# Turning the second group of v by DMA transposes instead of on TensorE, in a fused cross-covariance attention and feed-forward kernel

## The chip, the cores and the metric

The kernel runs on one core of a Trainium2 chip. A core has five engines with an instruction queue each: TensorE (PE, with weight loads of its own, PEld), VectorE (DVE), ScalarE (ACT), GpSimd (POOL) and SyncE (SP). SP only issues DMAs and waits; ACT and POOL issue DMAs too. All queues feed the same 16 DMA engines. An instruction starts when its engine has come to it and the semaphores that it waits for have been raised, so a waiting instruction holds up all that stands behind it on the same engine.

The metric is the device time of one execution in microseconds (us). Before the change it is 720.22 us, the median of three runs (720.19 to 720.47).

## The reference

B = 4 batches of N = 6080 rows and C = 256 channels; the feed-forward part has 2048 hidden units. Cut to what matters:

```python
qn = q / (norm(q, axis=1) + 1e-6);  kn = k / (norm(k, axis=1) + 1e-6)
s = kn.transpose(0, 2, 1) @ qn / tau          # (B, 256, 256): channels by channels
a = exp(s - s.max(-1));  a /= a.sum(-1) + 1e-9
x = (v @ a).reshape(B * N, 256)
h = x @ w_in                                   # (24320, 2048)
out = (s_ * maximum(h, 0)**2 + b_) @ w_out     # (24320, 256)
```

The scores are over channels, so a batch has one 256 x 256 matrix `a`, for which all rows of its q and k are read first. All of q, k, v and out are float32 in memory; the kernel computes in float16 with float32 sums.

## The kernel before

The kernel folds each batch's `a` into w_in: `wa = a @ w_in` (256 x 2048, held in float16), so that the hidden layer is `v @ wa` and x is never made. The 24,320 rows of v are cut into 48 groups of 512 rows (the last one has 256). A group needs `vT`, its rows turned so that channels lie on the partitions, since TensorE contracts over partitions.

**Before the steps (0 to 39 us).** POOL loads q and k of batch 0 in chunks, casting to float16 on the way; PE sums the scores (`Gram.mm`, L142), ACT and DVE square and fold for the norms. Then come w_in in three parts, v of group 0, v of group 1 (L418), the four parts of w_out (L424), v of group 2 (L426), and two scalars, all on POOL's queue. `keep_busy` (L438) gives PE idle products while it waits for loads. The softmax of batch 0 and the first part of its fold into w_in follow, and group 0's v is turned on PE (`transpose_v(0)`, L464).

**The steps.** The main loop (L797) has 48 x 16 steps and a tail; step s belongs to group s // 16. In a step PE multiplies one 128-wide block of `wa` with the group's `vT` (`mm1`, L605: two matmuls of 512 columns, into `h_ps`, of which there are two buffers of two blocks each). At every second step ACT applies the relu (L615) to two blocks. The squares (L626 on ACT, L628 on DVE) make `g`. The second product of a group runs some steps later among the first products of the next one: for group 0 and the last one plainly (`plain_mm2`, L677, group 0's from step 11 on), for the others with seven products in place of eight (L773), which needs sums of w_out's blocks (`combine_w`, L492 to L498) and of g's (`sums_of`, L699 to L705).

**Side work.** `at_step(s, f)` hangs a piece of work behind step s (L513); after the products and relus of a step all that hangs there is issued, in the order in which it was hung (L829). The first lines that use it place the rest of batch 0's fold (L521), the casts of w_out (L530, steps 7, 14, 18 and 24), the row sums of w_out (L532), and the loads of v (L540): groups 3 and 4 at step 2, group 5 at step 18, then one a group. The next batches' q and k, their scores, norms and softmax hang there as well (L546 to L572). The order on each engine is the order of issue: `po` keeps it.

**How v is turned.** There are two ways in the code. `transpose_v` (L366) has PE turn eight 128 x 128 blocks into a PSUM tile of the pool `ps_o` (three buffers, shared with the second products), and DVE copies them to `vT` (L374). `crossbar_v` (L377) has SP issue four DMA transposes (L383), each of which turns 128 rows of 256 channels straight into `vT`. Group 0 goes by the first way ahead of the steps, group 1 by the first way at step 12, and every group g from 2 on by the second way at step (g - 2) * 16 + 6. Since SP has hardly anything else to do, a transposing DMA is issued as soon as its v has landed and its `vT` is free, however late the step is at which it hangs.

**Buffers.** `v16` has four (`vpool`), `vT` three (`vtpool`). A buffer goes to the next load when the one that held it is released. POOL's DMAs take turns on eight semaphores, so that a load is issued when the one eight before it has landed.

Of the kernel before, what the change touches and what calls it, by code (L numbers as in the profile page):

```python
# [16 lines left out]
def kernel(  # L17
# [36 lines left out]
    def po(ins):  # L54

        tc.keep_in_program_order(ins)
        return ins
# [294 lines left out]
    def group(g):  # L352
        t0 = g * TG
        return t0, min(TG, NT - t0) // P
# [3 lines left out]
    def load_v(g):  # L358
        t0, nj = group(g)
        v16 = vpool.tile([P, TG // P, C], FP16, tag="v16", name="v16")  # L360
        po(nc.gpsimd.dma_start(  # L361
            out=v16[:, :nj, :],
            in_=v_flat[t0 : t0 + nj * P, :].rearrange("(p j) c -> p j c", j=nj)))
        v_tiles[g] = v16

    def transpose_v(g):  # L366
        _, nj = group(g)
        v16 = v_tiles.pop(g)
        vT_ps = ps_o.tile([P, CH, TG], FP16, tag="o_ps", name="vT_ps")
        for j in range(nj):  # L370
            for ch in range(CH):
                po(nc.tensor.transpose(vT_ps[:, ch, ts(j, P)], v16[:, j, ts(ch, P)], ident16))
        vT = vtpool.tile([P, CH, TG], FP16, tag="vT", name="vT")
        po(nc.vector.tensor_copy(out=vT[:, :, : nj * P], in_=vT_ps[:, :, : nj * P]))  # L374
        vT_tiles[g] = vT

    def crossbar_v(g):  # L377

        _, nj = group(g)
        v16 = v_tiles.pop(g)  # L380
        vT = vtpool.tile([P, CH, TG], FP16, tag="vT", name="vT")
        for j in range(nj):
            po(nc.sync.dma_start_transpose(out=vT[:, :, ts(j, P)], in_=v16[:, j, :]))  # L383
        vT_tiles[g] = vT
# [128 lines left out]
    def at_step(s, f):  # L513
        side.setdefault(int(s), []).append(f)
# [23 lines left out]
    for g in range(NG):  # L538
        if g >= 3:
            at_step(max(g - 4, 0) * FT + 2, lambda g=g: load_v(g))  # L540
        if g >= 1:
            if g == 1:
                at_step(12, lambda g=g: transpose_v(g))
            else:
                at_step((g - 2) * FT + 6, lambda g=g: crossbar_v(g))
    for b in range(1, B):  # L546
# [250 lines left out]
    for s in range(NS + FT):  # L797
        g, m = divmod(s, FT)
# [66 lines left out]
```

## Time and profile before

| what | value |
|---|---|
| median of three runs | 720.22 us |
| the profiled execution's own time | 720.22 us |
| its span, first to last instruction | 718.5 us |
| PE busy | 699.4 us, 97% |
| DVE busy | 625.9 us, 87% |
| ACT busy | 544.5 us, 76% |
| eight PE transposes of group 1 (L372) | from 48.49 us, 219 ns each, pipelined |
| DVE's copy of them (L374) | 49.13 us, 0.69 us |
| step 16, the first use of group 1's vT (L605) | 51.10 us |
| DMA transposes (L383) | 182, median 3.2 us from issue to landing, 2.3 to 8.7 |
| POOL's DMA queue (q0) | 26,064 packets, 43.40 MB |
| SP's DMA queue (q1) | 63,072 packets, 38.43 MB |

A row of the timeline gives start, duration, engine, line, operation, what is written and read, and, in brackets, how long the engine had been idle and what released it. PE's matmuls overlap: the duration of one is longer than the distance to the next, so the distance (the pitch) is what it costs. For a DMA the time to landing counts from its issue to the last of its 16 completion marks. "SPq" stands for SP's queue, whose rows are the issues, not the transfers. The trace also holds a record for each packet of a DMA, with its queue, start, duration and size.

### The profile page before, as it was taken

How to read it: one execution, taken by the hardware profiler on the slowest of the kernel's cores; microseconds unless marked ns; L12 is line 12 of the kernel's file. 1: busy time of each engine (PE TensorE's matmuls, PEld its weight loads, DVE VectorE, ACT ScalarE, POOL GpSimd, SP SyncE). 2: the span in 40 equal slices, each digit the busy share in tenths (PEclk: the TensorE clock that was granted, in tenths of full speed). 3: DMA queues.
4: the chain of work that ended last, by engine and by line, in shares of the span. 5: the costliest groups of instructions: out<-in, count | busy, mean ns of one | idle time of the engine just before them, and what ended most of it. 6: DMA issues, size and time to landing. Idle time of an engine off the chain costs nothing.

```text
span 718.5 us, 17642 instructions
## 1 busy us (share of the span) xinstructions
PE 699.4 (97%) x7481; PEld 505.0 (70%) x7481; DVE 625.9 (87%) x879; ACT 544.5 (76%) x588; POOL 109.8 (15%) x189
## 2 busy tenths in 40 slices
PE   4799999999999999999999999999999999999998
PEld 3556777776677777777677777777668777777777
DVE  4779999998889999999888899999887888888886
ACT  4489877887777777788777777778877777777875
POOL 4532332201201222111110222110000000000000
PEclk9999999999999999999999999999999999999999
DMA  9999999547565979443973777844423333321202
GB/s 237 207 259 148 172 166 149 110 103 134 103 105 120 153 133 144 105 96 75 152 155 63 139 136 125 154 93 83 105 65 75 92 71 74 97 59 46 83 30 75
DMA packets 89791, 84.27 MB, mean 117 GB/s; under 512 B 59664, under 2 KB 64848, under 8 KB 89712
## 3 DMA queue, kind: packets, MB, share of 16 engines
q0 software_dynamic: 26064, 43.40, 37.7%
q1 hardware_dynamic: 63072, 38.43, 21.5%
q8 instruction: 59, 0.97, 0.5%
q10 hardware_dynamic: 576, 1.31, 0.5%
q14 instruction: 20, 0.16, 0.1%
HBM read 78.91 MB, written 24.90 MB: 144 GB/s over the span
## 4 chain that ended last, share of the span: by engine, by line
PE 92%; DMA 4%; ACT 1%; DVE 1%; POOL 0%; issue 0%; ACTq 0%; POOLq 0%
PE h_ps L605 45%; PE o_ps L773 40%; PE s_ps L142 4%; PE wa_ps L309 2%; DMA qk<-in_q_dram 2%; DMA qk<-in_k_dram 1%; DMA w_in<-in_moe_w_in_dram 1%; ACT r L615 1%; PE o_ps L651 0%; POOL qk L126 0%; PE o_ps L677 0%; ACT g L626 0%; PE idle_ps L442 0%; DVE o_sb L633 0%; DVE sq L162 0%
## 5 line engine op out<-in xcount | busy, mean ns | idle before, releaser
L615 ACT ACTIVATE r<-h_ps 128x1024 f16<-128x1024 f32 (+1 forms) x384 | 387.6, 1013 | 146.9 <-PE h_ps L605 145.0
L605 PE MATMUL h_ps<-vT,wa 128*128 128x512 f16 (+7 forms) x1632 | 451.9, 364 | 0.6 <-ACT r L615 0.4
L773 PEld LDWEIGHTS <-S 128*128 128x128 f16 x2944 | 197.9, 98 | 85.1 <-DVE S L699 0.4
L773 PEld LDWEIGHTS <-g 128*128 128x128 f16 x2208 | 155.0, 98 | 74.1
L628 DVE TENSOR_TENSOR g<-r 128x2048 f16<-128x2048 f16 (+2 forms) x150 | 174.7, 1165 | 15.1 <-ACT r L615 14.9
L773 PE MATMUL o_ps<-T,S 128*128 128x128 f16 x2208 | 183.2, 219 | 0.3 <-DVE S L699 0.2
L605 PEld LDWEIGHTS <-wa 128*128 128x128 f16 x1632 | 136.0, 98 | 21.4 <-issue 1.0
L773 PE MATMUL o_ps<-w_out,g 128*128 128x128 f16 x1472 | 134.2, 219 | 0.3 <-DVE u L633 0.3
L633 DVE SCALAR_TENSOR_TENSOR o_sb<-o_ps,s_out,u 128x256 f32<-128x256 f32 x138 | 66.4, 481 | 47.6 <-PE o_ps L773 45.1
L626 ACT ACTIVATE g<-r 128x1024 f16<-128x1024 f16 (+1 forms) x97 | 100.4, 1035 | 0.2
L142 PE MATMUL s_ps<-qk 128*128 128x256 f16 (+1 forms) x384 | 70.0, 283 | 14.0 <-ACT qk L133 8.7
L361 POOL DMA_DIRECT2D v<-in_v_dram x48 | 31.3, 656 | 263.0 <-DMA vT<-v 199.5
L633 DVE SCALAR_TENSOR_TENSOR u<-o_ps,s_out,rowconst 128x256 f32<-128x256 f32 x138 | 65.9, 478 | 0.0
L773 PE MATMUL o_ps<-w_out,S 128*128 128x128 f16 x736 | 63.4, 219 | 0.0
L773 PE MATMUL o_ps<-N,g 128*128 128x128 f16 x736 | 63.4, 219 | 0.0
L188 POOL DMA_DIRECT2D f<-f x30 | 26.3, 877 | 225.8 <-DVE f L178 167.0
L165 ACT ACTIVATE sq<-qk 128x1024 f16<-128x1024 f16 (+3 forms) x49 | 50.4, 1033 | 10.3 <-DMA qk<-in_k_dram 6.3
L701 DVE TENSOR_TENSOR S<-S,g 128x2048 f16<-128x2048 f16 (+1 forms) x47 | 56.4, 1201 | 1.3
L699 DVE TENSOR_TENSOR S<-g 128x2048 f16<-128x2048 f16 (+1 forms) x47 | 56.0, 1192 | 0.0
L705 DVE TENSOR_TENSOR S<-g,S 128x2048 f16<-128x2048 f16 x46 | 55.9, 1216 | 0.0
L703 DVE TENSOR_TENSOR S<-g 128x2048 f16<-128x2048 f16 x46 | 55.9, 1215 | 0.0
L142 PEld LDWEIGHTS <-qk 128*128 128x128 f16 (+1 forms) x384 | 32.9, 101 | 19.8 <-DVE qk L132 8.1
(75 smaller groups left out, 324.3 us busy)
## 6 DMA issues: line engine op xcount, KB each, us to landing
out_dram<-o_sb SPq DMA_DIRECT2D x46, 512.0 KB, 3.0
v<-in_v_dram POOLq DMA_DIRECT2D x47, 256.0 KB, 4.7
qk<-in_k_dram POOLq DMA_DIRECT2D x42, 256.0 KB, 6.0
qk<-in_q_dram POOLq DMA_DIRECT2D x42, 256.0 KB, 7.2
f<-f POOLq DMA_DIRECT2D x30, 128.0 KB, 3.0
vT<-v SPq DMA_TRANSPOSE x182, 3.2
w<-in_moe_w_out_dram POOLq DMA_DIRECT2D x4, 512.0 KB, 11.4
raw<-in_q_dram ACTq DMA_DIRECT2D x2, 512.0 KB, 6.6
```

The costliest lines, as they stand in the source:

```text
L142: po(nc.tensor.matmul(self.s_ps[:, ch, :], kc[:np_, j, ts(ch, P)], qc[:np_, j, :], start=(c == 0 and j == 0 and ch == 0), stop=(c == len(s ...
L165: po(nc.scalar.activation(out=st["sq"][:np_, 1, js, :], in_=kc[:np_, js, :], func=AF.Square))
L605: po(nc.tensor.matmul(dst, wa[:, ci, ts(m, P)], src, start=(ci == 0), stop=(ci == CH - 1), skip_group_check=True))
L615: po(nc.scalar.activation(out=r16[:, :, i % 2, :n], in_=h_tiles.pop((g, i))[:, :, :n], func=AF.Relu))
L626: po(nc.scalar.activation(out=dst, in_=src, func=AF.Square))
L628: po(nc.vector.tensor_mul(dst, src, src))
L633: po(nc.vector.scalar_tensor_tensor(out=dst, in0=src, scalar=s_out, op0=ALU.mult, in1=add, op1=ALU.add))
L699: po(nc.vector.tensor_add(T[1], A21, A22))
L701: po(nc.vector.tensor_sub(T[2], T[1], A11))
L703: po(nc.vector.tensor_sub(T[3], A11, A21))
L705: po(nc.vector.tensor_sub(T[4], A12, T[2]))
L773: po(nc.tensor.matmul(st[name][:, j, :], a()[:, i, ts(j, P)], w[:, i, :], start=first, stop=last, skip_group_check=True))
```

## The change

One line: where group 1's v is turned on PE at step 12, four DMA transposes are hung at step 0.

```diff
@@ -540,7 +540,7 @@
             at_step(max(g - 4, 0) * FT + 2, lambda g=g: load_v(g))
         if g >= 1:
             if g == 1:
-                at_step(12, lambda g=g: transpose_v(g))
+                at_step(0, lambda g=g: crossbar_v(g))
             else:
                 at_step((g - 2) * FT + 6, lambda g=g: crossbar_v(g))
```

`transpose_v` then serves group 0 alone. What else moves with it: group 1's `v16` is released at step 0 in place of step 12, and thus ahead of group 2's (step 6) in place of behind it; its `vT` is taken at step 0; the pool `ps_o` has one tile less to give at step 12; and SP has four DMAs more, ahead of group 2's.

## The prediction

> **What bounds the kernel now.** I read the page first, then the chain of waits of 48 to 60 us, the order of time around the two places that the change touches, then the DMA side.
>
> The page says that the whole run is TensorE's, and that the DMA engines are full for the first eight of 40 slices (18 us each):
>
> ```profile
> PE 699.4 (97%) x7481; PEld 505.0 (70%) x7481; DVE 625.9 (87%) x879; ACT 544.5 (76%) x588; POOL 109.8 (15%) x189
> ...
> DMA  9999999547565979443973777844423333321202
> ```
>
> What PE loses anywhere is lost at the end, unless it waited there anyway. Its gaps between 51 and 75 us, start to start, are 0.10, 0.30 and 0.56 us behind ACT (to 59 us) and 1.12 us behind DVE (70 to 75); later it is dense. The order of time shows the operation removed, its two neighbours and the first use of its result (start, duration, engine, line, operation):
>
> ```profile
> 31.83 0.55 POOL L361 DMA_DIRECT2D v<-in_v_dram  x1
> ...
> 48.49 0.61 PE L372 MATMUL vT_ps<-ident,v 128*128 128x128 f16 x8
> 48.94 1.03 PE L605 MATMUL h_ps<-vT,wa 128*128 128x512 f16 x4
> 49.00 10.35 SPq L383 DMA_TRANSPOSE vT<-v  x8
> 49.13 0.69 DVE L374 COPY vT<-vT_ps 128x1024 f16<-128x1024 f16 x1
> ...
> 51.10 1.03 PE L605 MATMUL h_ps<-vT,wa 128*128 128x512 f16 x4
> ...
> 59.35 0.53 POOL L361 DMA_DIRECT2D v<-in_v_dram  x1 [9.55 <-DVE acc L476]
> ```
>
> The load of group 1's v is issued at 31.83. Step 16, the first product of group 1, runs at 51.10. The eight crossbar transposes from 49.00 are those of groups 2 and 3. How long loads and transposes take there, from issue to landing (v1; the first transpose of group 2; its third and fourth; a transpose at 562 us, where the queues are empty):
>
> ```profile
> v<-in_v_dram POOLq DMA_DIRECT2D x1, 256.0 KB, 9.9
> ...
> L383 SPq DMA_TRANSPOSE vT<-v x1: 1275/1275/1275, 49.0 to 49.0; - x1
> DMA to landing us min/median/max: 8.3/8.3/8.3
> ...
> L383 SPq DMA_TRANSPOSE vT<-v x2: 1247/1248/1250, 51.6 to 52.9; - x2
> DMA to landing us min/median/max: 5.9/6.4/6.9
> ...
> DMA to landing us min/median/max: 2.3/2.3/2.3
> ```
>
> So v1 lands at 41.7 (31.83 + 9.9). Group 2's transposes, issued 49.0, 50.3, 51.6 and 52.9, land at 57.3, 57.6, 58.5 and 58.8: all together, just when POOL's last load of this stretch (q, issued 49.27, 7.7 us to landing) is in at 57.0. In the stretches from 44 and 50 us (busy PE, PEld, DVE, ACT, POOL, clock, DMA share, GB/s) the DMA engines are full; at 58 they are not:
>
> ```profile
> 44.00:46.00 2.00, 2.00 (x11) 0.88 (x9) 1.46 (x3) 2.00 (x3) 0.76 (x2) 1.00 0.99 322
> 50.00:52.00 2.00, 2.00 (x15) 1.22 (x14) 1.38 (x2) 2.00 (x3) 0.00 (x0) 1.00 1.13 211
> 58.00:60.00 2.00, 1.60 (x12) 0.91 (x10) 1.97 (x4) 2.00 (x4) 0.65 (x2) 1.00 0.45 68
> ```
>
> The trace's packet records say why. POOL's loads go in packets of 2 or 4 KB, 0.17 to 0.19 us each; a transpose in 256 packets of 256 B and 32 of 4 B, some 0.02 us each, so 18 on each of 16 engines. The first packet of group 2 starts at 52.87, 3.9 us after its issue. From 53 to 54 us the transposes move 105 packets, the loads 103: one for one, so 26 KB beside 178 KB. Only when the loads run dry do they speed up (646 in the microsecond from 57).
>
> **The change, part by part.** *Removed:* eight PE transposes, 0.45 us of the chain at 48.65, and one DVE copy of 0.69. The relu behind them (49.57, ACT idle 1.2 us before it, released by PE) would start 0.45 earlier, and ACT is gapless from there to 59. In itself a gain of 0.45 us. The copy's 0.69 has no price: DVE idles 0.8 behind it. The PSUM tile has one taker next, the row constant's product at 63.5, with nothing to wait for either way.
>
> *Added:* four DMA transposes on SP. SP's queue is idle from its first loads on (one wait of 47.4 us, for v2), so the four are issued from 41.7, when v1 is in, at 41.7, 43.0, 44.3 and 45.5. Behind them on SP stand group 2's four, which wait for v2 (49.0) anyway.
>
> *When they land* decides. Lower bound, the row at 562 us: 45.5 + 2.3 = 47.8, in time for step 16, which could then run at 50.65. Nearest row: group 2's transposes, the same instructions in the same full queues 7 us later. First packet 3.9 us after the issue: 45.6. One for one with packets of 0.17 us, the 72 packets on an engine take 72 x 0.19 = 13.7 us, to 59.3, unless the loads run dry before. The loads' last landing, 57.0 now, moves by the turns that the transposes take: some 62 on the slowest engine where 22 are now, 40 x 0.02 = 0.8 us, to 57.8. The last ten packets and the receipt then take 0.4: 58.2. Upper bound, nothing moves until the loads are dry: group 2's fourth landing of 58.8, and 1.0 for the added turns, 59.8. I take 58.2, by the nearest row. In bandwidth alone it looks free: 256 KB beside 200 to 370 KB in a microsecond.
>
> *The stall.* Step 16 needs all four pieces (a product streams all 512 columns). It moves from 51.10 to 58.25: **+7.15 us**. Behind it in PE's order wait group 0's second products; behind those the relus of group 1 on ACT, and there the casts of w_out. DVE has 8 us of row sums and weight sums that it does meanwhile. The 0.45 is swallowed, as PE would merely wait longer.
>
> *The TensorE clock.* PE then has 7.6 us without work (50.65 to 58.25). The granted clock reads 1.00 throughout, but the matmuls' pace tells more: x8 of 128x256 take 1.87 us after the 6.93 us of idleness at the start, 1.03 later:
>
> ```profile
> 6.93 1.87 PE L142 MATMUL s_ps<-qk 128*128 128x256 f16 x8 [6.93 <-ACT qk L133]
> 10.58 4.76 PE L142 MATMUL s_ps<-qk 128*128 128x256 f16 x24 [1.78 <-ACT qk L133]
> 15.84 1.03 PE L142 MATMUL s_ps<-qk 128*128 128x256 f16 x8 [0.50 <-DMA qk<-in_q_dram]
> ```
>
> Their pitch is 0.213 us until 14.6 and 0.109 after. Gaps of up to 1.5 us later in that stage leave it at 0.109; no row has a long gap after warm work. Bounds: 0, and 2.85 us (half of all 5.7 us run at the slow pace). The stall of 7.6 is nearest to the 6.93 at the start. I take the second burst alone, 4.0 us at half pace: **+2.0 us**. The Trainium skill, "TensorE: Matmul & The Clock Gate", Part 1, says that about 3.4 us of idleness returns the array to half rate, and that about 3.4 us of work restores it. By it the price would be an estimated 1.7 us, and the sum 0.3 lower.
>
> *Given back:* with ACT and DVE caught up, the gaps behind ACT at 52 to 59 us go: **-0.95**. Those at 70 to 75 stay: they begin with the relu of step 31, which DVE awaits at 65.67 already.
>
> *Buffers:* v's buffers come free in the order of release. Now load 5 (59.35) takes group 2's and waits for its last transpose (58.8); then it takes group 1's, free at 58.2: no cost, nothing to gain. With four transposes more in SP's ring, group 2 lands at 60 to 61, needed by step 32, at 64.6 now and some 73 then; group 3, which meets the next loads, by 75, needed by step 48 at some 89. Either may slip 10 us unseen; beyond that the same stall begins again.
>
> *Sum:* 7.15 + 2.0 - 0.95 = **+8.2 us**. The profiled execution took 720.22 us, of which 718.5 are span; it equals the median of the three. So 728.4.
>
> A rule for the place of a transpose: the Trainium skill, "VectorE: DVE Perf Modes", Rules for kernel authors, has TensorE do a 128x128 transpose if PSUM will do as a destination, and the crossbar otherwise; the table in its section The three transpose paths gives 390 against 1309 ns. The rows here are farther apart: 0.45 us for all eight on PE, 5.9 to 8.3 us to landing for one crossbar piece under load. By that table's figures the eight blocks of the four pieces would take an estimated 10.5 us, to 52.2, and give a stall of an estimated 1.1 us and a time of 721.3.
>
> **The rivals.**
>
> 1. *Hidden in time.* The transposes run as in empty queues and land by 48. Then only the 0.45 remains: 719.8, not slower. It decides if the fourth piece lands before 50.65, 5.1 us after its issue. For it: other loads land between w_out's at 320 GB/s, so the engines can move more than 200. Against it: 5.9 us was the best of group 2, in its last, and that one profited from the loads' end at 57. Even with every gap before 59 regained it comes to 718.8.
>
> 2. *Late, but PE stays fast.* The pace of 0.109 survives 7.6 us of idleness. 726.4. For it: no row shows a warm array going slow. Against it: the start.
>
> 3. *Half late.* More packets get through per turn while w_out's plain rows pass (40 to 47 us), and the last piece lands at 52 to 57: 721 to 726, the lower end without a slow clock.
>
> 4. *A second stall.* Group 2's pieces, 72 packets on each engine later, also come late, or the slow pace lasts longer: 732 to 736. Against it: ten microseconds of room.
>
> **How the numbers follow.** A measurement of this kernel tells from no change about 0.2%, 1.4 us. Likeliest case 0.60 (own range 726.5 to 731, from landings of 57 to 59.8 and a clock price of 1 to 2.85); late with a fast clock 0.17; half late 0.08; hidden 0.11, of which 0.03 gain over 1.4 us; second stall 0.04. Slower 0.89, same 0.08, faster 0.03. The range from 722.5 to 732 leaves out the hidden case, the second stall and a third of the half late: 0.18.
>
> **What would show it.** In the changed profile: transposes on SP from 41.7 with 8 us or more to landing; the wait of L605 at step 16 put down to the DMA of vT, at some 58; PE's digits in slices 3 and 4 down; matmuls of 512 columns at a pitch near 0.43 instead of 0.216 for 4 us after it; from 80 us on the same rows, 8 us later. It is wrong if the fourth piece lands before 51, or if step 16 waits on something else.

## The result and the profile after

The changed kernel takes 729.35 us (median of four runs, 729.31 to 730.51) beside 720.35 us of the kernel before on the same chip: a ratio of 1.0129, with a 95% interval of 1.0111 to 1.0146. Forecast were 728.4 us and a range of 722.5 to 732. The profiled execution took 729.34 us, its span 727.6 (720.22 and 718.5 before).

Two lines of the page before, the shares of PE in slices of 18 us and the first products with their 0.6 us of waiting:

```profile
PE   4799999999999999999999999999999999999998
...
L605 PE MATMUL h_ps<-vT,wa 128*128 128x512 f16 (+7 forms) x1632 | 451.9, 364 | 0.6 <-ACT r L615 0.4
```

The page of the changed kernel: PE's busy time is almost what it was (700.6 in place of 699.4 us), the digits of slices 3 and 4 are down, and the first products now wait 8.1 us:

```profile
PE 700.6 (96%) x7473; PEld 504.9 (69%) x7473; DVE 625.3 (86%) x878; ACT 544.7 (75%) x588; POOL 109.8 (15%) x189
...
PE   4777999999999999999999999999999999999998
...
DMA  9998599644862988643875587944333333321201
...
L605 PE MATMUL h_ps<-vT,wa 128*128 128x512 f16 (+7 forms) x1632 | 453.2, 365 | 8.1 <-DMA vT<-v 7.6
```

The changed kernel's chain of waits from 46 to 64 us goes from SP's fourth issue straight to step 16 (start, duration, what):

```profile
45.12 1.29 SPq L383
46.40 0.04 issue
46.44 11.87 DMA vT<-v
58.31 0.14 issue
58.45 1.86 PE h_ps L605 x4
60.31 0.85 PE o_ps L677 x4
```

Its timeline has the twelve transposes of groups 1 to 3 in one row from 41.74, and names the landing as what ends PE's wait and, through PE, ACT's:

```profile
41.74 17.82 SPq L383 DMA_TRANSPOSE vT<-v  x12
...
58.45 1.86 PE L605 MATMUL h_ps<-vT,wa 128*128 128x512 f16 x4 [7.63 <-DMA vT<-v]
...
60.35 1.02 ACT L615 ACTIVATE r<-h_ps 128x1024 f16<-128x1024 f32 x1 [8.35 <-PE h_ps L605]
```

A piece is one of a group's four DMA transposes (128 rows). Group 1's first and fourth piece, from issue to landing:

```profile
L383 SPq DMA_TRANSPOSE vT<-v x1: 1280/1280/1280, 41.7 to 41.7; - x1
...
DMA to landing us min/median/max: 8.2/8.2/8.2
...
L383 SPq DMA_TRANSPOSE vT<-v x1: 1327/1327/1327, 46.4 to 46.4; - x1
...
DMA to landing us min/median/max: 11.9/11.9/11.9
```

Stretches of the changed kernel (busy PE, PEld, DVE, ACT, POOL, clock, DMA share, GB/s). PE has nothing to do from 56 to 58 us, and the granted clock is 0.50 from there to 62. The DMA engines are as full as before in the stretch from 44 us (1.01 for 0.99), and in the one from 58 us, where they had emptied before, they are still full (1.18 for 0.45):

```profile
44.00:46.00 2.00, 2.00 (x11) 0.88 (x9) 1.46 (x3) 2.00 (x3) 0.78 (x2) 1.00 1.01 333
...
56.00:58.00 2.00, 0.00 (x0) 0.00 (x0) 2.00 (x6) 0.00 (x0) 0.00 (x0) 0.50 1.25 168
58.00:60.00 2.00, 1.55 (x4) 0.58 (x5) 0.70 (x2) 0.00 (x0) 1.13 (x3) 0.50 1.18 182
60.00:62.00 2.00, 2.00 (x8) 1.03 (x7) 0.00 (x0) 1.65 (x2) 2.00 (x4) 0.50 0.85 108
62.00:64.00 2.00, 2.00 (x15) 1.30 (x13) 0.00 (x0) 1.27 (x3) 0.04 (x1) 0.97 1.10 191
```

The packet records, counted by the microsecond, show how the pieces move beside the loads (packets of all 16 engines, the changed kernel):

```
from us          46   47   48   49   50   51   52   53   54   55   56   57   58
POOL's loads     98  119   84   98  103   95  106   89  105  107   78    9    0
transposes       68  119   84   99  101   95  106   97   97  110  289  565  933
```

The first packet starts at 46.05, 4.3 us after the first issue. From 47 to 56 the transposes move as many packets as the loads, to within ten, and only when the loads run dry do they go faster. The starts of the same products in the two kernels (in us, and the shift):

| place | before | after | shift |
|---|---|---|---|
| step 16, first product | 51.10 | 58.45 | 7.35 |
| step 20, first product | 53.80 | 62.83 | 9.03 |
| step 26, first product | 58.99 | 67.83 | 8.84 |
| step 48, first product | 80.80 | 89.64 | 8.84 |
| product 1601 of 1632 | 700.54 | 709.38 | 8.84 |
| span | 718.5 | 727.6 | 9.1 |

All of it is lost by step 20; 0.2 us comes back by step 26, and from there on the two run alike. Some 0.26 us more is lost between the last products and the end of the span. It is there in every run below in which DMAs turn group 1 (0.24 to 0.27 us) and hardly in the two in which they do not (0.05); its cause is open.

### The profile page after: what moved, and what is told of

It reads as the page before. It is cut to its first block, busy times and chain, and to the rows that moved or that the text cites. A ratio compares the mean times of both kernels' runs of the same rounds, so it can differ in the third digit from the quotient of the medians.

```text
span 727.6 us, 17633 instructions
## 1 busy us (share of the span) xinstructions
PE 700.6 (96%) x7473; PEld 504.9 (69%) x7473; DVE 625.3 (86%) x878; ACT 544.7 (75%) x588; POOL 109.8 (15%) x189
## 4 chain that ended last, share of the span: by engine, by line
PE 90%; DMA 6%; DVE 1%; POOL 1%; ACT 1%; SPq 1%; issue 1%; POOLq 0%; ACTq 0%
PE h_ps L605 44%; PE o_ps L773 39%; PE s_ps L142 4%; DMA qk<-in_q_dram 3%; DMA vT<-v 2%; PE wa_ps L309 1%; DMA v<-in_v_dram 1%; SPq L383 1%; POOL qk L126 1%; PE o_ps L651 0%; PE o_ps L677 0%; ACT r L615 0%; ACT g L626 0%; DVE o_sb L633 0%; DVE sq L162 0%
## 5 line engine op out<-in xcount | busy, mean ns | idle before, releaser
L633 DVE SCALAR_TENSOR_TENSOR o_sb<-o_ps,s_out,u 128x256 f32<-128x256 f32 x138 | 66.4, 481 | 47.9 <-PE o_ps L773 45.4
```

The costliest lines, as they stand in the source:

```text
L633: po(nc.vector.scalar_tensor_tensor(out=dst, in0=src, scalar=s_out, op0=ALU.mult, in1=add, op1=ALU.add))
```

## The experiments

The theory: a crossbar piece is cut into packets of 256 B, which take turns with the packets of POOL's loads, one for one; so the pieces land late, PE waits and then works at half the clock. Rivals: the pieces are slow of themselves at this place; nothing of them gets through until the loads run dry; the slow work after the wait has another cause.

**Idle products while PE waits.**

```diff
+    at_step(15, lambda: keep_busy(30, w_in16[:, 0, :P], w_in16[:, 0, :NW]))
```

> The changed kernel with 30 idle products of 512 columns on PE behind step 15 (30 x 0.2155 = 6.5 us of the 7.6 us that PE waits), so that PE is never without work for more than 1.5 us. Theory (the array goes slow while it waits): the landing of group 1's last piece stays at 58.3 and PE goes on at 58.4 with a pitch of 0.216 from its first matmul; 1.9 us are saved less what ACT then takes back (up to 0.3): 727.4 to 727.8. Rival (the slow 4 us after the wait have another cause, such as weights or buffers): the pitch is 0.43 again and the time 729.3.

Measured: 727.87 us (ratio 1.0095 to before, 1.0082 to 1.0109), 1.5 us less than the changed kernel. The timeline has the idle products, and step 16 behind them; below it is the stretch from 58 us:

```profile
50.68 6.64 PE L442 MATMUL idle_ps<-w_in 128*128 128x512 f16 x30
...
58.71 1.02 PE L606 MATMUL h_ps<-vT,wa 128*128 128x512 f16 x4 [1.39 <-DMA vT<-v]
...
58.00:60.00 2.00, 1.29 (x8) 0.81 (x9) 0.73 (x2) 0.23 (x1) 0.87 (x2) 1.00 1.24 185
```

The four products after the wait take 1.02 us in place of 1.86, and the granted clock stays at 1.00 (0.50 in the same stretch of the changed kernel). From step 16 to step 20 PE needs 2.60 us here, 4.38 in the changed kernel: the slow clock costs 1.78. Step 16 starts 0.26 later here, and 0.12 is lost to a gap behind ACT; that leaves the 1.4 by which the spans differ. The clock is shown as the cause.

**Two buffers for v: no later loads beside the pieces.**

```diff
-    vpool = pool("vpool", 4)
+    vpool = pool("vpool", 2)
```

> The changed kernel with two buffers for v in place of four. The load of group 3's v then waits until group 1's pieces have landed, and all later loads stand behind it on POOL, so nothing but w_out and group 2's v lies beside the pieces, and the loads run dry at 49.3. Theory (the pieces get one small packet for each packet of a load, until the loads run dry): 15 to 20 of the 72 turns are done by then, the rest takes 1.0 us: the last piece lands at 50.3 to 50.8 in place of 58.3, PE waits 0 to 0.3 us and stays fast: 719.8 to 720.6; up to 2 us more if the first q and k of batch 1, now some 6 us later, come late for step 26. Rival (the pieces are slow of themselves at this place): they land at 58 again, 729.

Measured: 736.3 us (731.6 to 737.23; ratio 1.0197, 1.0171 to 1.0222). The pieces did what the theory says: the fourth, issued at 46.4, lands at 51.3, half a microsecond later than reckoned, and PE goes on at 51.40. The time did not, for a wait that the expectation had named but priced too low (the first two lines are the fourth piece, the others rows of the timeline):

```profile
L383 SPq DMA_TRANSPOSE vT<-v x1: 1247/1247/1247, 46.4 to 46.4; - x1
...
DMA to landing us min/median/max: 4.9/4.9/4.9
...
51.40 1.02 PE L605 MATMUL h_ps<-vT,wa 128*128 128x512 f16 x4 [0.57 <-DMA vT<-v]
51.82 0.54 POOL L361 DMA_DIRECT2D v<-in_v_dram  x1 [10.62 <-DMA vT<-v]
...
57.77 0.54 POOL L361 DMA_DIRECT2D v<-in_v_dram  x1 [5.41 <-DMA vT<-v]
...
58.82 0.55 POOL L126 DMA_DIRECT2D qk<-in_q_dram  x1
...
64.85 0.58 PE L142 MATMUL s_ps<-qk 128*128 128x256 f16 x2 [4.71 <-DMA qk<-in_q_dram]
```

Group 4's load waits for group 2's pieces, too (57.77), and batch 1's first q and k stand behind it: PE waits 4.7 us behind step 26, again goes slow (granted clock 0.50 from 61.67 to 68.50), and the shift is 6.8 us by step 64. Some 7.3 us more are lost by 146 us and 1.7 by 420; their causes are open. So the pieces' lateness is shown to come from the loads, and the loads cannot simply be put off.

**Three buffers for v.**

```diff
-    vpool = pool("vpool", 4)
+    vpool = pool("vpool", 3)
```

> As the last, with three buffers for v: group 3's v still goes beside the pieces, group 4's and all behind it wait. Theory: the loads run dry one load later, at 50.8; the last piece lands at 51.8 to 52.3, PE waits 1.5 us in place of 7.6 and stays fast: 721 to 722. Rival (slow of themselves): 729.

Measured: 721.7 us (ratio 1.0016, 1.0007 to 1.0025), as expected. The fourth piece lands at 51.95:

```profile
52.09 1.02 PE L605 MATMUL h_ps<-vT,wa 128*128 128x512 f16 x4 [1.40 <-DMA vT<-v]
```

One buffer fewer takes 8.0 us off the change (its products run 0.8 us behind those of the kernel before, in place of 8.84), by keeping five loads out of the pieces' way. The three landings (51.3 with group 2's load as the last beside them, 51.95 with group 3's, 58.3 with all) follow the last load's landing: 49.6, 51.1, 58.3.

**Group 1 not turned.** Its products take group 0's turned v, so the turning of group 1 is left out and its rows of the output are not the reference's.

```diff
-                at_step(0, lambda g=g: crossbar_v(g))
+                at_step(0, lambda: (v_tiles.pop(1), vT_tiles.__setitem__(1, vT_tiles[0])))
```

> Group 1's v is not turned at all; its products take group 0's turned v. This leaves out the turning of group 1 and makes its 512 rows of the output those of group 0's v with the same weights. It prices what the change could have brought at most had the pieces been in time. Theory: only the 0.45 us of PE's eight transposes goes: 719.6 to 720.0 beside 720.3 of before. Rival (the copy on DVE or the PSUM tile cost something, too): 719.2 or less.

Measured: 720.13 us beside 720.56 (ratio 0.9992, 0.9983 to 1.0001). Step 16 starts at 50.62 in place of 51.10; products 1601 stand 0.4 us apart (700.13 and 700.54). The 0.45 of the prediction is all that could be had, and too little to tell by the time alone.

**Group 1's v loaded two loads earlier.**

```diff
     load_v(0)
+    load_v(1)
     load_w_in(NW, 2 * NW)
     load_w_in(2 * NW, Dff)
     w_out_rows = moe_w_out.rearrange("(fo p) d -> p fo d", p=P)
-    load_v(1)
```

> The changed kernel with the load of group 1's v two loads earlier (right behind group 0's, ahead of the second and third part of w_in), so that it lands at 38.0 in place of 41.7 and the pieces are issued 3.7 us earlier; POOL's loads as a whole last as long. Theory (one small packet for each packet of a load: 72 turns of 0.19 us from 4.4 us after the first issue): the last piece lands at 56.2 to 56.8 in place of 58.3, PE still goes slow after it: 727.3 to 728.0. Rival (nothing gets through until the loads run dry): 58.3 and 729.3.

Measured: 726.89 us (ratio 1.0086, 1.0071 to 1.0102). The fourth piece is issued at 41.7, takes 14.1 us and lands at 55.8, while the loads run until 60.15:

```profile
L383 SPq DMA_TRANSPOSE vT<-v x1: 1247/1247/1247, 41.7 to 41.7; - x1
...
DMA to landing us min/median/max: 14.1/14.1/14.1
```

From 50 to 56 us 86 to 111 transpose packets start in each microsecond beside 92 to 112 of the loads. So turns are taken, and not merely the end of the loads awaited: the last rival falls. The landing and the time lie 0.4 us below what was expected; the clock is at 0.50 from 56.04 to 59.45.

**The four pieces at step 12**, behind group 2's on SP.

```diff
-                at_step(0, lambda g=g: crossbar_v(g))
+                at_step(12, lambda g=g: crossbar_v(g))
```

> The changed kernel with the four pieces of group 1 hung at step 12 in place of step 0, so that they stand behind group 2's four on SP, which wait for group 2's v until 49.3. Theory: 144 packets on each engine, of which some 21 are through when the loads run dry at 57.3; the last piece of group 1 lands at 59.5 to 60.3 and PE goes on 1.4 us later than in the changed kernel: 730.6 to 731.3. Rival (the place in SP's order is of no matter): 729.3.

Measured: 734.06 us (ratio 1.0184, 1.0170 to 1.0198), 3 us above what was expected: PE goes on 4.0 us later than in the changed kernel, not 1.4. The place on SP matters, and more than the theory's sum has it:

```profile
59.05 0.53 POOL L361 DMA_DIRECT2D v<-in_v_dram  x1 [9.02 <-DVE acc L476]
59.57 0.54 POOL L126 DMA_DIRECT2D qk<-in_k_dram  x1
...
62.46 1.01 PE L605 MATMUL h_ps<-vT,wa 128*128 128x512 f16 x2 [11.60 <-DMA vT<-v]
```

What the sum left out is SP's own pace: an issue takes 1.3 us, so the eighth goes out at 58.28, later than the loads run dry (last landing 57.23). Group 2's pieces free its buffer at 58.50, the next loads are issued from 59.05, and the last piece meets these: its packets of 256 B are through by 59.98, but those of 4 B follow only from 60.56 to 62.00, among the loads' packets, which start at 60.29. It lands at 62.3, 4.0 us after its issue.

**The later loads held back, four buffers.** Group 0's buffer (no longer given up in `transpose_v`) and the fourth one are held until step 1, so that group 3's v takes group 1's buffer and waits for its pieces; group 4's load stands behind batch 1's first q and k.

```diff
-        v16 = v_tiles.pop(g)
+        v16 = v_tiles[g]
...
     transpose_v(0)
+    kept = [vpool.tile([P, TG // P, C], FP16, tag="v16", name="v16")]
+    po(nc.gpsimd.memset(kept[0][:, 0, 0:1], 0.0))
...
-            at_step(max(g - 4, 0) * FT + 2, lambda g=g: load_v(g))
+            at_step({3: 2, 4: 17}.get(g, (g - 4) * FT + 2), lambda g=g: load_v(g))
...
+                at_step(1, lambda: [po(nc.gpsimd.memset(t[:, 0, 0:1], 0.0)) for t in (v_tiles.pop(0), kept.pop())])
```

> The changed kernel with POOL's loads from group 3's v on held back until group 1's pieces have landed: four buffers for v as before, but group 3's v takes group 1's buffer, and group 4's load stands behind those of batch 1's first q and k. Theory: the pieces land at 51.3 as with two buffers, PE goes on at 51.4, 0.3 later than in the kernel before, and the first q and k, now from 52.4, land by 59 and 61, in time for steps 26 and 29, so that there is no second wait: 720.3 to 720.9. If they are late, 725 or more.

Measured: 720.6 us beside 720.46 (ratio 1.0000, 0.9991 to 1.0009). The fourth piece lands at 51.06, PE goes on at 51.19 and does not wait for q and k:

```profile
51.62 0.53 POOL L361 DMA_DIRECT2D v<-in_v_dram  x1 [10.05 <-DMA vT<-v]
...
52.66 0.56 POOL L126 DMA_DIRECT2D qk<-in_q_dram  x1
...
59.77 0.38 PE L142 MATMUL s_ps<-qk 128*128 128x256 f16 x2
```

The whole loss of the change is undone with the crossbar still turning group 1, by the order of POOL's loads alone.

**Both: held back, and group 1's v early.** The edits of the last run and of the early load.

> The last two together: group 1's v loaded two loads earlier and the loads from group 3's v on held back. Theory: from 42.4 to 49.5 some 38 turns are done, the other 34 packets take 0.6 us: the last piece lands at 50.2 to 50.6, in time for step 16 at 50.65; the whole gain of 0.4 us of the run without turning remains: 719.8 to 720.2, the fastest of all. If one packet for one does not hold with the pieces beside w_in's and w_out's loads, they land at 51.3 and the time is that of the last.

Measured: 721.43 us (ratio 1.0014, 1.0006 to 1.0023): a miss. The fourth piece lands at 52.34, later than without the early load:

```profile
52.48 1.02 PE L608 MATMUL h_ps<-vT,wa 128*128 128x512 f16 x4 [1.58 <-DMA vT<-v]
```

The pieces took their turns (84 packets beside 86 of the loads from 42 to 43 us, 36 of 72 turns done by 49.5 as reckoned), but the loads fell behind: group 2's v lands at 51.31 in place of 49.66. Its stretches show where:

```profile
41.00:43.00 2.00, 2.00 (x11) 0.90 (x10) 1.26 (x2) 1.83 (x3) 0.00 (x0) 1.00 1.05 362
43.00:45.00 2.00, 2.00 (x11) 0.88 (x9) 1.46 (x4) 1.93 (x4) 0.00 (x0) 1.00 1.10 255
45.00:47.00 2.00, 2.00 (x11) 0.92 (x10) 1.78 (x3) 1.93 (x3) 0.00 (x0) 1.00 1.08 148
```

**The kernel before with the early load.** Is it the order of the loads that holds them up in the last run, or the pieces beside them?

> The kernel before (group 1's v turned on PE) with group 1's v loaded two loads earlier, a control for the two runs with that order, in which w_out's last part landed at 50.1 in place of 47.9 and the DMA engines moved 150 to 170 GB/s from 45 to 47 us in place of 275. Theory (the pieces' packets between w_out's rows hold the loads up): without pieces w_out's last part lands at 48 and group 2's v at 49 again, the stretch from 45 to 47 moves 260 to 290 GB/s, and the time is that of the kernel before, 720.2 to 720.8. Rival (the order of the loads does it, whatever stands beside them): 50 and 51, and 150 to 200 GB/s.

Measured: 720.35 us (ratio 0.9990, 0.9979 to 1.0001). The same stretches of this run:

```profile
41.00:43.00 2.00, 2.00 (x11) 0.92 (x10) 1.23 (x2) 1.82 (x3) 0.53 (x1) 1.00 1.03 360
43.00:45.00 2.00, 2.00 (x11) 0.94 (x10) 1.49 (x3) 1.93 (x4) 0.54 (x1) 1.00 1.02 334
45.00:47.00 2.00, 2.00 (x11) 0.89 (x10) 1.78 (x4) 1.93 (x3) 0.76 (x2) 1.00 1.06 287
```

Without pieces beside them the loads move 334 and 287 GB/s where they moved 255 and 148, w_out's last part lands at 47.9 in place of 50.2, and group 2's v at 48.95. The changed kernel with the early load, which differs from this run only in how group 1 is turned, has 251 and 167 GB/s in these stretches and w_out's last part at 50.07. So it is the pieces that hold the loads up, far beyond the 0.02 us of a packet.

No version that was run is faster than the kernel before by more than the measurement can tell; the held-back one equals it.

## Why the prediction was right

- *What bounds the kernel and what is removed*: right. The run without the turning gives 0.4 us for the 0.45, and relu's start at 49.11 in the changed kernel is 0.46 earlier than before.
- *When the pieces land*: right, 58.31 for 58.2, and by the mechanism named. That it fits to 0.1 us is luck: the loads' last landing went to 58.29, predicted 57.8, and the pieces finished with it and not 0.4 behind, so that two errors cancel. First packet 4.3 us after the issue, for 3.9.
- *The stall*: 7.35 for 7.15; 0.11 is the landing, the rest the 0.14 from landing to PE's start where 0.05 was taken.
- *The clock*: 1.78 for 2.0, shown by the run with idle products. The choice of the row at the start of the kernel was right, against the warm rows with short gaps (the longest of them, ahead of 23.41, is 1.1 us, not the 1.5 of the prediction). The rule of the Trainium skill, "TensorE: Matmul & The Clock Gate", Part 1, on which the prediction draws, gave an estimated 1.7, which is nearer. But 2.0 and 1.5 us without work before the fall were enough in two of the runs (last section), where the page has some 3.4. That the granted clock "reads 1.00 throughout" hid it: the clock's records begin at 14.7 us in the kernel before, and what lies ahead of the first record reads as 1.00. In the changed kernel the 0.50 stands in the stretches.
- *Given back*: mis-sized, 0.29 in place of 0.95. The gaps of 0.10 and 0.30 shrink to one of 0.10, but that of 0.56 ahead of step 26 is there in every run, after a wait or not. The prediction took it for lateness that ACT carries along from step 15; that it comes back behind every wait points to the order of ACT's own work from step 19 to 24 (relus, squares, a cast of w_out). No run tests it.
- *Sum*: 7.35 + 1.78 - 0.29 = 8.84, the shift of all products from step 26 on, for 8.2; with the 0.26 at the end 9.1, the difference of the spans.
- *Buffers*: group 5's load went from 59.35 to 58.87, at no cost. It waits for DVE's sums (L476) in both kernels, as the row in the prediction says, and not for a transpose, as its text has it. No stall followed: groups 2 and 3 landed by 59.7 and 63.0, far ahead of their steps.
- *The rivals*: hidden in time, late with a fast clock and half late each came about only in a run that was altered for it: with the held-back loads, the idle products and the three buffers.
- *The rule on where to transpose* (the Trainium skill, "VectorE: DVE Perf Modes", Rules for kernel authors) spoke against the change, and the sign agrees. The 1309 ns for a 128x128 block, in the page's section The three transpose paths, are not what a piece of two such blocks takes here, 8.2 to 11.9 us to landing beside loads. With the loads held back the crossbar costs nothing (720.6 us): what decides here is what lies beside the pieces.

## What to carry to other kernels

Ask of a transfer that a change adds not how many bytes it has, but how many packets, and what stands in the same DMA engines while it runs: 72 packets an engine took 12 us, because most of them waited for a load's packet each. What must land soon is helped by keeping loads that nobody needs yet out of its way, and one buffer fewer can do that; but look at what is queued behind the load that is held. And a wait of TensorE costs more than its length once the clock falls: 1.8 us here.

## What the runs showed of the hardware that was not expected

- Crossbar pieces between w_out's rows slow the loads themselves: from 45 to 47 us the engines moved 148 GB/s in place of 287, and w_out's last part came 2.3 us later. In the changed kernel, where they meet only the end of w_out, group 2's v is 0.3 us late. The packet records show that both kinds were held up, and not that one took the other's turns: from 44 to 47 us 25 to 60 packets of each kind start in a microsecond, where the loads alone had 93 to 112, and those of 4 KB that start from 45 to 46 us take 0.56 us in the mean in place of 0.19. Why is open.
- The first packet of a piece comes 3.9 to 4.4 us after its issue beside full queues.
- By the clock's records the clock changes in steps of 3.41 us counted from its first rise: its first stretch at 1.00 is 40.96 us long in the changed kernel, 12 steps, and 37.55 in the run at step 12, 11 steps. It fell at 55.29 in the changed kernel, some 4.5 us after PE's last product, for 6.83 us; 5.4 us after it in the run with the early load; only 2.0 us after it in the run at step 12 (at 52.89) and 1.5 us in the run with two buffers (at 61.67). Idle stretches of 1.4 to 1.6 us (three runs) left it at 1.00. So how long PE may wait depends on where the wait lies in that count. How much idleness a step must hold is not settled: by the modelled ends of the products, 1.9 and 2.0 us in one step brought the clock down in two runs, and 2.0 left it up in the run with the early load. The price differs less: the products from step 16 to 20 took 1.7, 1.8 and 2.0 us more than with a fast clock in the early, the changed and the step-12 kernel.
